# Splitting the FFN columns over the two row groups, with weight loads over 128 partitions

## The chip, the cores and the metric

The kernel runs on one NeuronCore of a Trainium2 chip. The metric is the device time of one execution in microseconds, median over runs. The kernel before takes 527.3 us (525.35 to 528.24, 3 runs). In the profile, PE is the matmul engine (TensorE), PEld its weight loading, DVE is VectorE, ACT is ScalarE, POOL is GpSimd and SP is SyncE, which issues transfers here and computes nothing. "SPq" is SP's instruction queue. The transfers of SP, ACT and POOL travel in different queues (in the page of the kernel before 17.79, 0.52 and 11.80 MB), but those of SP and POOL share the same 16 DMA engines. A packet is the piece of a transfer that the records list one by one; in the new weight loads it is one row of 4608 bytes for one partition.

## The reference

Two residual blocks follow each other on 2048 tokens of 576 values, in bfloat16: a spectral filter after a layer norm, then a gated FFN after a layer norm.

```python
def _A_ref(x, w_r, w_i):                      # S, D = 2048, 576
    X = jnp.fft.rfft2(x.astype(jnp.float32), axes=(-2, -1))
    X = X * (w_r + 1j * w_i)
    return jnp.fft.irfft2(X, s=(S, D), axes=(-2, -1)).astype(jnp.bfloat16)

def _B_ref(x, w_gate, w_up, w_down):          # 576x4608, 576x4608, 4608x576
    return (_gelu(x @ w_gate) * (x @ w_up)) @ w_down

h  = x + _A_ref(_layernorm(x), A_w_r, A_w_i)
h2 = h + _B_ref(_layernorm(h), B_w_gate, B_w_up, B_w_down)
```

## The kernel before

The spectral block is a chain of matmul stages on PE (forward transforms, 16 groups with a 16-point stage on both sides of the filter, an inverse transform), lasting until about 91 us. The FFN then goes through four blocks of 512 tokens. The contraction over 576 values is cut into 9 chunks of 64. A matmul then has 64 rows, and two of them, in the upper and in the lower row group, run at the same time: in the profile below a gate/up matmul of 64 rows and 512 columns takes 108.1 ns, which is 0.211 ns per column, a down matmul of 128 rows and only 288 columns 122.9 ns, 0.427 per column. In the kernel before the gate weights lie in partitions 0 to 63 and the up weights in 64 to 127; one row group computes gate, the other up. For this the normalized input HT is stored twice, so that each chunk is there for both row groups; slots 5 to 8 of HT are copies of slots 0 to 4 in the other half.

```python
# weights: two transfers per 512 columns, each to 64 partitions, rows of 1024 bytes
for j in range(9):
    f0, f1 = 512 * j, 512 * j + 512
    P.dma(POOL, WGU[0:64, :, f0:f1],   wgv[:, :, f0:f1], f"wg{j}", w=[("WG", j, 0)])
    P.dma(SP,   WGU[64:128, :, f0:f1], wuv[:, :, f0:f1], f"wu{j}", w=[("WG", j, 1)])
# WD shares its memory with the spectral stage, so its loads wait for the end of that
for j in range(9):
    P.dma(POOL, WD[:, 4 * j:4 * j + 4, :], wdv[:, 4 * j:4 * j + 4, :], f"wd{j}", w=[("WD", j)])
...
# first FFN block: PE transposes the input, DVE evicts, SP copies into the other half
P.op(DVE, ... v.tensor_copy(HT0[:, 0:5, t0:t1], PS[...]) ...)
P.dma(SP, HT0[0:64, 5:9, t0:t1],   HT0[64:128, 0:4, t0:t1], f"tr{c}", ...)
P.dma(SP, HT0[64:128, 5:9, t0:t1], HT0[0:64, 1:5, t0:t1],   f"tr{c}", ...)
...
def gu(n, tb, f):                    # 36 column tiles f per token block
    b0 = 2 * (n % 3)                 # three pairs of PSUM banks
    for kt in range(9):
        for o in range(2):           # o = 0 gate, upper rows; 1 up, lower rows
            h0, sl = 64 * o, (GT, UT)[o][kt]
            P.op(PE, ... t.matmul(bank(b0 + o), WGU[h0:h0 + 64, kt, 128 * f:128 * f + 128],
                                  HT[h0:h0 + 64, sl, :], start=(kt == 0), stop=(kt == 8)) ...)
    ...
    P.op(ACT, ... GL = gelu(bank b0)); P.op(DVE, ... AT[:, f, :] = GL * bank b0 + 1)
```

SP's queue holds, in this order: the inputs, constants and filter weights, the tables DT and IT for the inverse transform, the nine up transfers, the copies into HT.

Of the kernel before, what the change touches and what calls it, by code (L numbers as in the profile page):

```python
# [4 lines left out]
BF16 = mybir.dt.bfloat16  # L5
# [5 lines left out]
KW = 290  # L11
ZW = 320
FF = 4608
NT = 16
# [268 lines left out]
def _build(nc, A_x, A_w_r, A_w_i, B_w_gate, B_w_up, B_w_down, out):  # L283
# [6 lines left out]
    top = nc.sbuf_top  # L290
    sb = SbufMap(nc, base, top)
    XO = sb.alloc("XO", [128, NT, D], BF16)
    WGU = sb.alloc("WGU", [128, 9, FF], BF16)
    HN = sb.alloc("HN", [128, 2, 640], BF16)
    IDT = sb.alloc("IDT", [128, 128], BF16)
    ST1 = sb.alloc("ST1", [128, NT, 2, 6], F32)
# [39 lines left out]
    YS = sb.alloc("YS", [128, 2, 2, KW], BF16)  # L336
    T1 = sb.alloc("T1", [128, 2, 2, KW], BF16)
    T2 = sb.alloc("T2", [128, 2, 2, KW], BF16)
    ZS = sb.alloc("ZS", [128, 2, 2, ZW], BF16)
    SQ = sb.alloc("SQ", [128, 2, D], BF16)  # L340
    sb.off = v_off
    AT = sb.alloc("AT", [128, 36, 512], BF16)
    HT1 = sb.alloc("HT1", [128, 9, 512], BF16)
    GL = sb.alloc("GL", [128, 2, 512], BF16)
    HTS = (HT0, HT1)

    PS = nc.alloc_psum_tensor("PS", [128, 4096], F32)
# [1 line left out]
    def bank(b, p0=0, p1=128, c0=0, c1=512):  # L349
        return PS[p0:p1, b * 512 + c0:b * 512 + c1]  # L350
# [182 lines left out]
    def st_B(i):  # L533
        g = GORD[i]
        sl = i % 2
        sp_ = 1 if g == 0 else 0
        for b, tabs in ((4, (0, 1)), (5, (1, 2))):
            for o in range(2):
                P.op(PE, lambda t, b=b, o=o, tb=tabs[o], sl=sl, sp_=sp_: t.matmul(bank(b, 0, 128, 0, K2), BT[:, sp_, tb, :], CUS[:, sl, o, 0:K2],  # L539
                                                                              start=(o == 0), stop=(o == 1)),  # L540
                     r=[("CU", sl) if o == 0 else ("SU", sl), "BT"], w=[("PS", b)])
        P.op(ACT, lambda a, sl=sl: a.activation(YS[:, sl, :, 0:K2], banks(4, 2, K2), ACTF.Copy), r=[("PS", 4), ("PS", 5)], w=[("Y", sl)])  # L542
        wk = wkeys[0 if 1 <= g < 9 else 1] + ["Wz", "Yz", "Zz"]
        P.op(DVE, lambda v, g=g, sl=sl: v.tensor_tensor(T1[:, sl, :, :], YS[:, sl, :, :], WS[:, g, :, :], op=ALU.mult), r=[("Y", sl)] + wk, w=[("T1", sl)])  # L544
        for pl in range(2):
            P.op(DVE, lambda v, g=g, sl=sl, pl=pl: v.tensor_tensor(T2[:, sl, pl, :], YS[:, sl, pl, :], WS[:, g, 1 - pl, :], op=ALU.mult),
                 r=[("Y", sl)] + wk, w=[("T2", sl, pl)])
        P.op(DVE, lambda v, sl=sl: v.tensor_tensor(ZS[:, sl, 0, 0:KW], T1[:, sl, 0, :], T1[:, sl, 1, :], op=ALU.subtract), r=[("T1", sl)], w=[("Z", sl, 0)])
        P.op(DVE, lambda v, sl=sl: v.tensor_tensor(ZS[:, sl, 1, 0:KW], T2[:, sl, 0, :], T2[:, sl, 1, :], op=ALU.add), r=[("T2", sl, 0), ("T2", sl, 1)], w=[("Z", sl, 1)])  # L549

    def st_V(i):
        g = GORD[i]
        sl = i % 2
        sp_ = 1 if g == 0 else 0
        zk = [("Z", sl, 0), ("Z", sl, 1), "Zz", "VT"]
        for c in range(2):
            for zp in range(2):
                P.op(PE, lambda t, c=c, zp=zp, sl=sl, sp_=sp_: t.matmul(bank(6, 0, 128, 256 * c, 256 * c + 256), ZS[:, sl, zp, 128 * c:128 * c + 128],  # L558
                                                                        VT[:, sp_, zp, :], start=(zp == 0), stop=(zp == 1)), r=zk, w=[("PS", 6)])
        for t_ in range(2):  # L560
            for zp in range(2):
                P.op(PE, lambda t, t_=t_, zp=zp, sl=sl, sp_=sp_: t.matmul(bank(7, 64 * t_, 64 * t_ + 64, 0, 128), ZS[:, sl, zp, 256:320],  # L562
                                                                         VT[:, sp_, zp, 128 * t_:128 * t_ + 128], start=(zp == 0), stop=(zp == 1)),
                     r=zk, w=[("PS", 7)])
        P.op(ACT, lambda a, g=g: a.activation(V[:, 0:4, :, g, :], bank(6).rearrange("p (k n e) -> p k n e", k=4, n=16), ACTF.Copy),  # L565
             r=[("PS", 6), "Vfree"], w=[("V", g)])
        P.op(DVE, lambda v, g=g: v.tensor_copy(V[:, 4, :, g, :], bank(7, 0, 128, 0, 128).rearrange("p (n e) -> p n e", n=16)),
             r=[("PS", 7), "Vfree"], w=[("Vt", g)])


    P.alias(["ATB", "J0", "J1", "ZD"] + [("ATS", c) for c in range(NT)], ["Vfree"])
    for i in range(NG + 2):
        if i < NG:
            st_D(i)
        if 1 <= i <= NG:
            st_B(i - 1)
        if i >= 2:
            st_V(i - 2)


    wgv = B_w_gate[:, :].rearrange("(t p) f -> p t f", p=64)
    wuv = B_w_up[:, :].rearrange("(t p) f -> p t f", p=64)
    wdv = B_w_down[:, :].rearrange("(c p) d -> p c d", p=128)
    for j in range(9):
        f0, f1 = 512 * j, 512 * j + 512
        P.dma(POOL, WGU[0:64, :, f0:f1], wgv[:, :, f0:f1], f"wg{j}", w=[("WG", j, 0)])
        P.dma(SP, WGU[64:128, :, f0:f1], wuv[:, :, f0:f1], f"wu{j}", w=[("WG", j, 1)])
    P.alias(ukeys + wkeys[0] + wkeys[1] + ["Wz", ("CU", 0), ("CU", 1), ("SU", 0), ("SU", 1)], [("WD", j) for j in range(9)])
    for j in range(9):
        P.dma(POOL, WD[:, 4 * j:4 * j + 4, :], wdv[:, 4 * j:4 * j + 4, :], f"wd{j}", w=[("WD", j)])  # L590
# [52 lines left out]
    def turn_dma(c):  # L643
        hs = c % 2
        q = c // 4
        HT = HTS[q % 2]
        for k in range(9):
            o = 128 * k if k < 5 else 64 + 128 * (k - 5)
            P.dma(SP, HT[:, k, 128 * (c % 4):128 * (c % 4) + 128], HN[:, hs, o:o + 128], f"tr{c}",
                  r=[("HN", hs, 0), ("HN", hs, 1)], w=[("HT", q % 2, c % 4, k)], transpose=True)  # L650
# [27 lines left out]
            turn_pe((c - 7) // 2)  # L678

    fdead = vkeys + ["DT", "IT", ("G", 0), ("G", 1), ("Y", 0), ("Y", 1), "Yz", "Zz", ("SQ", 0), ("SQ", 1)]  # L680
    fdead += [("T1", a) for a in range(2)] + [(n_, a, b_) for n_ in ("T2", "Z") for a in range(2) for b_ in range(2)]
    fnew = ([("AT", f) for f in range(36)] + [("GL", 0), ("GL", 1)] + [("HT", 1, i, k) for i in range(4) for k in range(9)])

    GT = (0, 5, 1, 6, 2, 7, 3, 8, 4)
    UT = (4, 0, 5, 1, 6, 2, 7, 3, 8)

    def gu(n, tb, f):
        b0 = 2 * (n % 3)
        HT = HTS[tb % 2]
        rk = [("HT", tb % 2, i, k) for i in range(4) for k in range(9)] + [("WG", f // 4, i) for i in range(2)]  # L690
        for kt in range(9):
            for o in range(2):
                h0, sl = 64 * o, (GT, UT)[o][kt]
                P.op(PE, lambda t, o=o, h0=h0, kt=kt, sl=sl, f=f, b0=b0, HT=HT: t.matmul(  # L694
                    bank(b0 + o), WGU[h0:h0 + 64, kt, 128 * f:128 * f + 128], HT[h0:h0 + 64, sl, :], start=(kt == 0), stop=(kt == 8)),
                    r=rk, w=[("PS", b0 + o)])
        if n == 0:
            st_N(NT - 1)
            P.alias(fdead, fnew)
        s2 = n % 2  # L700
        P.op(ACT, lambda a, s2=s2, b0=b0: a.activation(GL[:, s2, :], bank(b0), ACTF.Gelu_apprx_tanh), r=[("PS", b0)], w=[("GL", s2)])  # L701
        P.op(DVE, lambda v, s2=s2, b0=b0, f=f: v.tensor_tensor(AT[:, f, :], GL[:, s2, :], bank(b0 + 1), op=ALU.mult),  # L702
             r=[("GL", s2), ("PS", b0 + 1)], w=[("AT", f)])

    def down(tb, p):
        b0 = 6 - 2 * (p % 2)
        c = 4 * tb + p
        for h in range(2):
            for f in range(36):
                P.op(PE, lambda t, b0=b0, h=h, f=f, p=p: t.matmul(bank(b0 + h, 0, 128, 0, 288), AT[:, f, 128 * p:128 * p + 128],  # L710
                                                                  WD[:, f, 288 * h:288 * h + 288], start=(f == 0), stop=(f == 35)),
                     r=[("AT", f), ("WD", f // 4)], w=[("PS", b0 + h)])
            P.op(DVE, lambda v, b0=b0, h=h, p=p, c=c: v.tensor_tensor(OS[:, p % 2, 288 * h:288 * h + 288], bank(b0 + h, 0, 128, 0, 288),  # L713
                                                                      XO[:, c, 288 * h:288 * h + 288], op=ALU.add),
                 r=[("PS", b0 + h), ("X", c)], w=[("OS", p % 2, h)])
            P.dma(SP, ov[:, c, 288 * h:288 * h + 288], OS[:, p % 2, 288 * h:288 * h + 288], f"so{p % 2}{h}", r=[("OS", p % 2, h)], w=[("OUT", p % 2, h)])

    for tb in range(4):
        for f in range(36):
            gu(36 * tb + f, tb, f)  # L720
            if tb == 0 and f == 20:
                ln2_a(3)
                ln2_b(3)
                ln2_c(3)
            if tb < 3 and f % 4 == 3 and f < 16:
                norm(4 * (tb + 1) + f // 4)
                turn_dma(4 * (tb + 1) + f // 4)
        for p in range(4):
            down(tb, p)
    P.op(SP, None, r=[("OUT", i, h) for i in range(2) for h in range(2)])  # L730
# [36 lines left out]
```

## Time and profile before

| what | value | view |
|---|---|---|
| time | 527.3 us | runs |
| span; PE busy | 526.9 us; 96% | page, part 1 |
| one FFN block, gate/up and down | 70.04 and 35.39 us | chain of waits |
| first gate/up matmul starts | 98.8 us | chain of waits |
| PE waits for the copies into HT | 8.1 us | waits |

From the page, the busy share in 40 slices of 13.2 us: each digit is tenths, PEclk is the granted clock in tenths, DMA the share of 16 DMA engines.

```profile
span 526.9 us, 10210 instructions
...
PE   7899898499999999999999999999999999999997
...
PEclk9999999699999999999999999999999999999999
DMA  8999999401110000011100000111000000000000
```

PE is full from slice 9 on; the DMA engines are full until slice 7. The dip of PE and of its clock lies at the border of the two stages. The next lines are from the chain of waits: start, length, what.

```profile
94.94 3.51 DMA HT_69<-HT_69
...
98.81 4.02 PE PS L694 x18
...
207.93 70.04 PE PS L694 x648
277.97 35.39 PE PS L710 x288
```

The first matmul of the FFN is released by a copy into HT. From the second block on there is no gap: 648 matmuls in 70.04 us are 108.1 ns each, two in parallel. The DMA engines in some stretches (the last two figures of a row are the busy share of 16 engines and GB/s):

```profile
core 0: us, PE busy (x) PEld busy (x) DVE busy (x) ACT busy (x) POOL busy (x), PEclk, DMA share, GB/s
20.00:40.00 20.00, 18.81 (x164) 13.48 (x163) 13.23 (x46) 11.16 (x23) 4.49 (x7) 1.00 1.06 215
40.00:60.00 20.00, 20.00 (x178) 14.36 (x176) 15.20 (x57) 12.36 (x25) 0.00 (x0) 1.00 1.06 233
60.00:85.00 25.00, 22.68 (x194) 16.80 (x193) 16.44 (x54) 18.37 (x41) 6.72 (x9) 1.00 1.09 265
85.00:99.00 14.00, 5.89 (x51) 4.33 (x50) 5.17 (x16) 6.04 (x15) 0.00 (x0) 0.83 0.94 223
```

And the issues of transfers, with the median time from issue to landing:

```profile
WGU<-in_B_w_gate_dram POOLq DMA_DIRECT2D x9, 576.0 KB, 25.8
WGU<-in_B_w_up_dram SPq DMA_DIRECT2D x9, 576.0 KB, 31.7
WD<-in_B_w_down_dram POOLq DMA_DIRECT2D x9, 576.0 KB, 18.0
...
DT<-c_dtab SPq DMA_DIRECT2D x1, 720.0 KB, 24.4
...
IT<-c_itab SPq DMA_DIRECT2D x1, 512.0 KB, 28.0
```

They stand in SP's queue ahead of the up weights, whose first packet came at 40.1 us; this will matter.

### The profile page before, as it was taken

The page shows a single profiled execution, that of the slowest core. Times are in us where ns is not written, and L with a number is a line of the kernel's source. Part 1 is how long each engine was busy: PE and PEld are TensorE (multiplying, and loading weights), DVE is VectorE, ACT ScalarE, POOL GpSimd, SP SyncE. Part 2 cuts the span into 40 slices and gives each one's busy share as a digit, 9 for nine tenths or more (in the row PEclk, how much of TensorE's full clock was granted, in tenths as well). Part 3 has the DMA queues.
Part 4 walks back from the last instruction along what each step waited for, and adds up shares of the span by engine and source line. Part 5 has one row for each costly group of instructions (what it writes and reads, how often), then busy time and mean ns, then how long its engine had stood idle before and what let it go on. Part 6 is the DMA issues. An engine that isn't in the chain of part 4 may idle for free.

```text
span 526.9 us, 10210 instructions
## 1 busy us (share of the span) xinstructions
PE 507.8 (96%) x4425; PEld 302.5 (57%) x4427; DVE 184.1 (35%) x428; ACT 152.8 (29%) x285; POOL 29.1 (6%) x49
## 2 busy tenths in 40 slices
PE   7899898499999999999999999999999999999997
PEld 3667576144444777444447774456677744444776
DVE  5677658044433111343331114433311133333111
ACT  5756578042343000223330002333300023333000
POOL 8800130000000000000000000000000000000000
PEclk9999999699999999999999999999999999999999
DMA  8999999401110000011100000111000000000000
GB/s 289 247 208 230 220 268 316 68 11 26 26 25 7 13 18 18 11 26 24 26 9 12 17 18 11 27 27 26 6 12 18 18 1 1 0 1 2 12 18 18
DMA packets 36812, 30.76 MB, mean 58 GB/s; under 512 B 21296, under 2 KB 32752, under 8 KB 36768
## 3 DMA queue, kind: packets, MB, share of 16 engines
q1 hardware_dynamic: 33312, 17.79, 14.8%
q0 software_dynamic: 3312, 11.80, 8.8%
q8 instruction: 35, 0.57, 0.5%
q10 hardware_dynamic: 144, 0.52, 0.3%
q14 instruction: 9, 0.07, 0.1%
HBM read 23.67 MB, written 2.36 MB: 49 GB/s over the span
## 4 chain that ended last, share of the span: by engine, by line
PE 88%; SPq 3%; DVE 3%; DMA 3%; ACT 2%; issue 1%; DVEq 0%; ACTq 0%
PE PS L694 51%; PE PS L710 27%; PE PS L525 4%; PE PS L601 3%; SPq L191 2%; DMA XO<-in_A_x_dram 2%; PE PS L539 1%; SPq L193 1%; PE PS L558 1%; ACT U L453 1%; DMA HT_69<-HT_69 1%; PE PS L610 1%; PE PS L562 1%; DVE XO L613 1%; DMA HT_84<-HN 0%
## 5 line engine op out<-in xcount | busy, mean ns | idle before, releaser
L701 ACT ACTIVATE GL<-PS 128x512 bf16<-128x512 f32 x144 | 85.8, 597 | 294.5 <-PE PS L694 293.0
L702 DVE TENSOR_TENSOR AT<-GL,PS 128x512 bf16<-128x512 bf16 x144 | 98.6, 687 | 167.1 <-ACT GL L701 167.1
L694 PE MATMUL PS<-HT_69,WGU 64*128 64x512 bf16 x1296 | 143.3, 380 | 8.2 <-DMA HT_69<-HT_69 8.1
L710 PE MATMUL PS<-WD,AT 128*128 128x288 bf16 x1152 | 141.8, 286 | 0.0
L694 PE MATMUL PS<-HT_84,WGU 64*128 64x512 bf16 x1296 | 140.2, 376 | 0.0
L710 PEld LDWEIGHTS PS<-WD,AT 128*128 128x128 bf16 x1152 | 112.4, 98 | 29.9 <-issue 1.7
L694 PEld LDWEIGHTS PS<-HT_69,WGU 64*128 64x128 bf16 x1296 | 70.8, 95 | 79.8 <-issue 11.7
L694 PEld LDWEIGHTS PS<-HT_84,WGU 64*128 64x128 bf16 x1296 | 62.6, 94 | 77.1 <-issue 0.5
L713 DVE TENSOR_TENSOR OS<-PS,XO 128x288 bf16<-128x288 f32 x32 | 14.6, 458 | 123.8 <-PE PS L710 123.8
L601 PE MATMUL PS<-DT,V 128*128 128x288 bf16 x160 | 22.0, 286 | 0.5 <-ACT V L565 0.5
L525 PE MATMUL PS<-FT,U 128*128 128x289 bf16 x160 | 22.3, 287 | 0.2 <-ACT U L453 0.2
L613 DVE SCALAR_TENSOR_TENSOR XO<-PS,XO 128x576 bf16<-128x576 f32 x16 | 12.1, 756 | 20.0 <-PE PS L610 19.8
L601 PEld LDWEIGHTS PS<-DT,V 128*128 128x128 bf16 x160 | 15.4, 98 | 4.3 <-issue 0.6
L525 PEld LDWEIGHTS PS<-FT,U 128*128 128x128 bf16 x160 | 14.4, 97 | 5.1 <-issue 0.4
L616 ACT ACTIVATE SQ<-XO 128x576 bf16<-128x576 bf16 x16 | 10.9, 682 | 15.3 <-DVE XO L613 15.1
L639 DVE TENSOR_SCALAR HN<-XO,TM,RS_59 128x576 bf16<-128x576 bf16 (+1 forms) x32 | 10.2, 360 | 8.8 <-DMA HT_84<-HN 6.4
L434 PE MATMUL PS<-ZD 128*128 128x512 bf16 x37 | 10.9, 447 | 1.5 <-POOL ZD L356 1.3
L558 PE MATMUL PS<-VT,ZS 128*128 128x256 bf16 x64 | 9.6, 271 | 2.4 <-DVE ZS L549 1.6
L405 DVE BATCH_NORM_STATS2 ST_53<-XO 128x6 f32<-128x288 bf16 x24 | 9.2, 443 | 5.5 <-DMA XO<-in_A_x_dram 5.5
L544 DVE TENSOR_TENSOR T_79<-YS,WS 128x580 bf16<-128x580 bf16 x16 | 7.4, 460 | 10.4 <-ACT YS L542 10.4
L603 ACT ACTIVATE GS<-PS 128x576 bf16<-128x576 f32 x16 | 10.2, 636 | 2.6 <-PE PS L601 2.6
L542 ACT ACTIVATE YS<-PS 128x578 bf16<-128x578 f32 x16 | 10.5, 655 | 1.5 <-PE PS L539 0.3
(57 smaller groups left out, 171.8 us busy)
## 6 DMA issues: line engine op xcount, KB each, us to landing
WGU<-in_B_w_gate_dram POOLq DMA_DIRECT2D x9, 576.0 KB, 25.8
WGU<-in_B_w_up_dram SPq DMA_DIRECT2D x9, 576.0 KB, 31.7
WD<-in_B_w_down_dram POOLq DMA_DIRECT2D x9, 576.0 KB, 18.0
out_dram<-OS SPq DMA_DIRECT2D x32, 72.0 KB, 1.6
XO<-in_A_x_dram SPq DMA_DIRECT2D x3, 576.0 KB, 8.0
HT_84<-HN SPq DMA_TRANSPOSE x72, 2.4
FT<-c_ftab SPq DMA_DIRECT2D x1, 725.0 KB, 12.5
DT<-c_dtab SPq DMA_DIRECT2D x1, 720.0 KB, 24.4
```

The costliest lines, as they stand in the source:

```text
L191: fn = lambda e: e.dma_start(out_ap, in_ap, transpose=True)
L434: P.op(PE, lambda t: t.matmul(bank(7), ZD[:, 0:128], ZD[:, :], start=True, stop=True), r=["ZD"], w=[("PS", 7)])
L525: P.op(PE, lambda t, b=b, o=o, dt=dt, g=g: t.matmul(bank(b, 0, 128, 0, K2), U[:, dt, g, :, :], FT[:, dt, o, 0:K2], start=(dt == 0), stop=( ...
L558: P.op(PE, lambda t, c=c, zp=zp, sl=sl, sp_=sp_: t.matmul(bank(6, 0, 128, 256 * c, 256 * c + 256), ZS[:, sl, zp, 128 * c:128 * c + 128], V ...
L601: P.op(PE, lambda t, b=b, h=h, kt=kt, c=c: t.matmul(bank(b, 0, 128, 0, 288), V[:, kt, c, :, :], DT[:, kt, 288 * h:288 * h + 288], start=(k ...
L613: P.op(DVE, lambda v, x2=x2, c=c: v.scalar_tensor_tensor(x2, banks(4, 2, 288), 1.0, x2, op0=ALU.mult, op1=ALU.add, accum_out=SB2[:, 0, c:c ...
L616: P.op(ACT, lambda a, sl=sl, c=c: a.activation(SQ[:, sl, :], XO[:, c, :], ACTF.Square, accum_out=SB2[:, 1, c:c + 1]), r=[("X", c)], w=[("S ...
L694: P.op(PE, lambda t, o=o, h0=h0, kt=kt, sl=sl, f=f, b0=b0, HT=HT: t.matmul(bank(b0 + o), WGU[h0:h0 + 64, kt, 128 * f:128 * f + 128], HT[h0 ...
L701: P.op(ACT, lambda a, s2=s2, b0=b0: a.activation(GL[:, s2, :], bank(b0), ACTF.Gelu_apprx_tanh), r=[("PS", b0)], w=[("GL", s2)])
L702: P.op(DVE, lambda v, s2=s2, b0=b0, f=f: v.tensor_tensor(AT[:, f, :], GL[:, s2, :], bank(b0 + 1), op=ALU.mult), r=[("GL", s2), ("PS", b0 + ...
L710: P.op(PE, lambda t, b0=b0, h=h, f=f, p=p: t.matmul(bank(b0 + h, 0, 128, 0, 288), AT[:, f, 128 * p:128 * p + 128], WD[:, f, 288 * h:288 * ...
L713: P.op(DVE, lambda v, b0=b0, h=h, p=p, c=c: v.tensor_tensor(OS[:, p % 2, 288 * h:288 * h + 288], bank(b0 + h, 0, 128, 0, 288), XO[:, c, 28 ...
```

## The change

The intent has two parts. First, the columns are split over the row groups: partitions 0 to 63 hold columns 0 to 2303 of gate and of up, partitions 64 to 127 hold columns 2304 to 4607 of both. Each transfer then fills all 128 partitions in runs of 4608 bytes, where before it filled 64 in runs of 1024. One call of `gu` makes two gate tiles, then two up tiles, in two sets of four PSUM banks. Second, the inverse 16-point stage `st_V` lags three groups behind instead of two, with three slots of ZS. The PSUM banks of `down` and the places where the next block is normalized were adapted to this; the cut below leaves that out.

```diff
-    WGU = sb.alloc("WGU", [128, 9, FF], BF16)
+    WGU = sb.alloc("WGU", [128, 2, 9, FF // 2], BF16)
...
-    ZS = sb.alloc("ZS", [128, 2, 2, ZW], BF16)
+    ZS = sb.alloc("ZS", [128, 3, 2, ZW], BF16)
...
-    for i in range(NG + 2):
+    for i in range(NG + 3):
...
-        if i >= 2:
-            st_V(i - 2)
+        if i >= 3:
+            st_V(i - 3)
...
-    for j in range(9):
-        f0, f1 = 512 * j, 512 * j + 512
-        P.dma(POOL, WGU[0:64, :, f0:f1], wgv[:, :, f0:f1], f"wg{j}", w=[("WG", j, 0)])
-        P.dma(SP, WGU[64:128, :, f0:f1], wuv[:, :, f0:f1], f"wu{j}", w=[("WG", j, 1)])
+    for kt in range(9):
+        for o, src in enumerate((B_w_gate, B_w_up)):
+            a = bass.AP(src.tensor, 64 * kt * FF, [[FF // 2, 2], [FF, 64], [1, FF // 2]])
+            P.dma((POOL, SP)[o], WGU[:, o, kt, :], a, f"wg{o}", w=[("WG", o, kt)])
...
+    def gu(tb, n):                       # 18 calls per token block
+        b0 = 4 * (n % 2)
+        for o in range(2):
+            for kt in range(9):
+                for h in range(2):       # h: row group and half of the columns
+                    h0, sl = 64 * h, (GT, UT)[h][kt]
+                    P.op(PE, ... t.matmul(bank(b0 + 2 * o + h), WGU[h0:h0 + 64, o, kt, 128 * n:128 * n + 128],
+                                          HT[h0:h0 + 64, sl, :], ...),
+                        r=rk + [("WG", o, k) for k in range(9)], ...)
...                                       # gelu and product for f = n and n + 18; GL has four slots
+    FORD = [f for f in range(36) if f % 18 != 17] + [17, 35]     # order of the down matmuls
```

The first gate matmul now waits for all nine gate transfers and the first up matmul for all nine up transfers; before, each tile waited for its own 512 columns.

More of the change, by code (lines that the diff above doesn't have):

```diff
@@ L343, in _build @@
     HT1 = sb.alloc("HT1", [128, 9, 512], BF16)
-    GL = sb.alloc("GL", [128, 2, 512], BF16)
+    GL = sb.alloc("GL", [128, 4, 512], BF16)
     HTS = (HT0, HT1)
@@ L547, in st_B @@
                  r=[("Y", sl)] + wk, w=[("T2", sl, pl)])
-        P.op(DVE, lambda v, sl=sl: v.tensor_tensor(ZS[:, sl, 0, 0:KW], T1[:, sl, 0, :], T1[:, sl, 1, :], op=ALU.subtract), r=[("T1", sl)], w=[("Z", sl, 0)])
-        P.op(DVE, lambda v, sl=sl: v.tensor_tensor(ZS[:, sl, 1, 0:KW], T2[:, sl, 0, :], T2[:, sl, 1, :], op=ALU.add), r=[("T2", sl, 0), ("T2", sl, 1)], w=[("Z", sl, 1)])
+        P.op(DVE, lambda v, sl=sl: v.tensor_tensor(ZS[:, i % 3, 0, 0:KW], T1[:, sl, 0, :], T1[:, sl, 1, :], op=ALU.subtract), r=[("T1", sl)], w=[("Z", i % 3, 0)])
+        P.op(DVE, lambda v, sl=sl: v.tensor_tensor(ZS[:, i % 3, 1, 0:KW], T2[:, sl, 0, :], T2[:, sl, 1, :], op=ALU.add), r=[("T2", sl, 0), ("T2", sl, 1)], w=[("Z", i % 3, 1)])
     def st_V(i):
         g = GORD[i]
-        sl = i % 2
+        sl = i % 3
         sp_ = 1 if g == 0 else 0
@@ L576, in _build @@
             st_B(i - 1)
-        if i >= 2:
-            st_V(i - 2)
-    wgv = B_w_gate[:, :].rearrange("(t p) f -> p t f", p=64)
-    wuv = B_w_up[:, :].rearrange("(t p) f -> p t f", p=64)
+        if i >= 3:
+            st_V(i - 3)
     wdv = B_w_down[:, :].rearrange("(c p) d -> p c d", p=128)
-    for j in range(9):
-        f0, f1 = 512 * j, 512 * j + 512
-        P.dma(POOL, WGU[0:64, :, f0:f1], wgv[:, :, f0:f1], f"wg{j}", w=[("WG", j, 0)])
-        P.dma(SP, WGU[64:128, :, f0:f1], wuv[:, :, f0:f1], f"wu{j}", w=[("WG", j, 1)])
+    for kt in range(9):
+        for o, src in enumerate((B_w_gate, B_w_up)):
+            a = bass.AP(src.tensor, 64 * kt * FF, [[FF // 2, 2], [FF, 64], [1, FF // 2]])
+            P.dma((POOL, SP)[o], WGU[:, o, kt, :], a, f"wg{o}", w=[("WG", o, kt)])
     P.alias(ukeys + wkeys[0] + wkeys[1] + ["Wz", ("CU", 0), ("CU", 1), ("SU", 0), ("SU", 1)], [("WD", j) for j in range(9)])
@@ L680, in _build @@
     fdead = vkeys + ["DT", "IT", ("G", 0), ("G", 1), ("Y", 0), ("Y", 1), "Yz", "Zz", ("SQ", 0), ("SQ", 1)]
-    fdead += [("T1", a) for a in range(2)] + [(n_, a, b_) for n_ in ("T2", "Z") for a in range(2) for b_ in range(2)]
-    fnew = ([("AT", f) for f in range(36)] + [("GL", 0), ("GL", 1)] + [("HT", 1, i, k) for i in range(4) for k in range(9)])
+    fdead += [("T1", a) for a in range(2)] + [(n_, a, b_) for n_ in ("T2", "Z") for a in range(3) for b_ in range(2)]
+    fnew = ([("AT", f) for f in range(36)] + [("GL", i) for i in range(4)] + [("HT", 1, i, k) for i in range(4) for k in range(9)])
@@ L684, in _build @@
     GT = (0, 5, 1, 6, 2, 7, 3, 8, 4)
     UT = (4, 0, 5, 1, 6, 2, 7, 3, 8)
-    def gu(n, tb, f):
-        b0 = 2 * (n % 3)
+    def gu(tb, n):
+        b0 = 4 * (n % 2)
         HT = HTS[tb % 2]
-        rk = [("HT", tb % 2, i, k) for i in range(4) for k in range(9)] + [("WG", f // 4, i) for i in range(2)]
-        for kt in range(9):
-            for o in range(2):
-                h0, sl = 64 * o, (GT, UT)[o][kt]
-                P.op(PE, lambda t, o=o, h0=h0, kt=kt, sl=sl, f=f, b0=b0, HT=HT: t.matmul(
-                    bank(b0 + o), WGU[h0:h0 + 64, kt, 128 * f:128 * f + 128], HT[h0:h0 + 64, sl, :], start=(kt == 0), stop=(kt == 8)),
-                    r=rk, w=[("PS", b0 + o)])
-        if n == 0:
-            st_N(NT - 1)
-            P.alias(fdead, fnew)
-        s2 = n % 2
-        P.op(ACT, lambda a, s2=s2, b0=b0: a.activation(GL[:, s2, :], bank(b0), ACTF.Gelu_apprx_tanh), r=[("PS", b0)], w=[("GL", s2)])
-        P.op(DVE, lambda v, s2=s2, b0=b0, f=f: v.tensor_tensor(AT[:, f, :], GL[:, s2, :], bank(b0 + 1), op=ALU.mult),
-             r=[("GL", s2), ("PS", b0 + 1)], w=[("AT", f)])
+        rk = [("HT", tb % 2, i, k) for i in range(4) for k in range(9)]
+        for o in range(2):
+            for kt in range(9):
+                for h in range(2):
+                    h0, sl = 64 * h, (GT, UT)[h][kt]
+                    P.op(PE, lambda t, o=o, h=h, h0=h0, kt=kt, sl=sl, n=n, b0=b0, HT=HT: t.matmul(
+                        bank(b0 + 2 * o + h), WGU[h0:h0 + 64, o, kt, 128 * n:128 * n + 128], HT[h0:h0 + 64, sl, :], start=(kt == 0), stop=(kt == 8)),
+                        r=rk + [("WG", o, k) for k in range(9)], w=[("PS", b0 + 2 * o + h)])
+            if o == 0 and tb == 0 and n == 0:
+                st_N(NT - 1)
+                P.alias(fdead, fnew)
+            for h in range(2):
+                f = n + 18 * h
+                s4 = 2 * (n % 2) + h
+                if o == 0:
+                    P.op(ACT, lambda a, s4=s4, b=b0 + h: a.activation(GL[:, s4, :], bank(b), ACTF.Gelu_apprx_tanh), r=[("PS", b0 + h)], w=[("GL", s4)])
+                else:
+                    P.op(DVE, lambda v, s4=s4, b=b0 + 2 + h, f=f: v.tensor_tensor(AT[:, f, :], GL[:, s4, :], bank(b), op=ALU.mult),
+                         r=[("GL", s4), ("PS", b0 + 2 + h)], w=[("AT", f)])
@@ L705, in down @@
+    FORD = [f for f in range(36) if f % 18 != 17] + [17, 35]
     def down(tb, p):
-        b0 = 6 - 2 * (p % 2)
         c = 4 * tb + p
         for h in range(2):
-            for f in range(36):
-                P.op(PE, lambda t, b0=b0, h=h, f=f, p=p: t.matmul(bank(b0 + h, 0, 128, 0, 288), AT[:, f, 128 * p:128 * p + 128],
-                                                                  WD[:, f, 288 * h:288 * h + 288], start=(f == 0), stop=(f == 35)),
-                     r=[("AT", f), ("WD", f // 4)], w=[("PS", b0 + h)])
-            P.op(DVE, lambda v, b0=b0, h=h, p=p, c=c: v.tensor_tensor(OS[:, p % 2, 288 * h:288 * h + 288], bank(b0 + h, 0, 128, 0, 288),
-                                                                      XO[:, c, 288 * h:288 * h + 288], op=ALU.add),
-                 r=[("PS", b0 + h), ("X", c)], w=[("OS", p % 2, h)])
+            b = 2 * p + h
+            for i, f in enumerate(FORD):
+                P.op(PE, lambda t, b=b, h=h, f=f, p=p, i=i: t.matmul(bank(b, 0, 128, 0, 288), AT[:, f, 128 * p:128 * p + 128],
+                                                                    WD[:, f, 288 * h:288 * h + 288], start=(i == 0), stop=(i == 35)),
+                     r=[("AT", f), ("WD", f // 4)], w=[("PS", b)])
+            P.op(DVE, lambda v, b=b, h=h, p=p, c=c: v.tensor_tensor(OS[:, p % 2, 288 * h:288 * h + 288], bank(b, 0, 128, 0, 288),
+                                                                    XO[:, c, 288 * h:288 * h + 288], op=ALU.add),
+                 r=[("PS", b), ("X", c)], w=[("OS", p % 2, h)])
@@ L716, in down @@
             P.dma(SP, ov[:, c, 288 * h:288 * h + 288], OS[:, p % 2, 288 * h:288 * h + 288], f"so{p % 2}{h}", r=[("OS", p % 2, h)], w=[("OUT", p % 2, h)])
     for tb in range(4):
-        for f in range(36):
-            gu(36 * tb + f, tb, f)
-            if tb == 0 and f == 20:
+        for n in range(18):
+            gu(tb, n)
+            if tb == 0 and n == 9:
                 ln2_a(3)
@@ L724, in _build @@
                 ln2_c(3)
-            if tb < 3 and f % 4 == 3 and f < 16:
-                norm(4 * (tb + 1) + f // 4)
-                turn_dma(4 * (tb + 1) + f // 4)
+            if tb < 3 and n % 2 == 1 and n < 8:
+                norm(4 * (tb + 1) + n // 2)
+                turn_dma(4 * (tb + 1) + n // 2)
         for p in range(4):
```

## The prediction

> What bounds the kernel now. The page gives a span of 526.9 us with PE busy 96%. By the chain of waits, the FFN matmuls (L694, L710) hold 78%, and from the second token block on they run at a floor: each block takes 70.04 us for 648 gate/up matmuls (108.1 ns each, two row groups overlapping) and 35.39 us for 288 down matmuls (122.9 ns each). The only loose time lies before the FFN and in its first block. (a) PE waits 8.1 us for the copies into HT (view of waits): the last HT eviction ends at 89.45 us, the last copy lands at 98.45, because SP's queue and the 16 DMA engines are full (DMA share 1.05 to 1.13 in the stretches from 20 to 90 us, at only 209 to 243 GB/s from 30 to 60 us, but 319 GB/s from 75 to 90). (b) After that idle time the granted clock is 0.54 from 99 to 105 us, worth about 2.8 us. (c) The inverse stage idles about 1.0 us at its first group. (d) DVE waits on HN cost PE 0.7 us in block one.
>
> What the change leaves. It has the same 2592 gate/up matmuls of 64x512 in alternating row groups, so 70.04 us per block stays; four GL slots and reordered banks only add slack. The down order reads its last two AT tiles last, so no new wait there. The lag of 3 should remove (c), about 1 us, and nothing in the periods of 2.51 us, where PE is full.
>
> What it changes is the weight loads. The intent is good: 1024-byte packets to half the partitions take a median 86 to 89 ns in the trace's packet records (11.7 GB/s per engine), whereas 4608-byte packets of the input load took 178 ns (25.9 GB/s). But the DRAM pattern of the new transfers starts with a dimension of 2. [...]
>
> Cost, an estimate from those durations: up is 9 x 64 packets of 4608 bytes per engine, 576 x 178 ns = 102 us; beside it the same engines carry one or two gate transfers (11 to 23 us) and their share of WD (72 packets, 13 us). Starting near 25 us, up lands at about 150 to 163 us. The HT copies queue behind it on SP, so the first gate matmul starts near 157 us instead of 98.8: all on the critical path, plus 58 us. The remaining 428 us stay, less 1.
>
> Prediction: 584 us, range 556 to 606; faster by over 2%: 0.10, within 2%: 0.15, slower by over 2%: 0.75.
>
> What would show it: DMA share drops to about 2/16 to 3/16 between 45 and 150 us at some 50 GB/s; SP's issues of WGU stall past 100 us; PE idle for 60 us at slice 8 to 11, then released by the HT copies or WGU; blocks two to four unchanged at 105.43 us each.
>
> What would make it wrong: if the transfers spread over all 16 engines after all, the weights land by about 62 us and WD by 83, the HT copies by 93, PE stays warm, and (a) to (d) give back 5 + 2.8 + 1 + 0.6 us: about 518 us, just under 2% faster. If two engines move more than 26 GB/s each, or carry fewer gate transfers, the loss is nearer 40 us.

What the estimate goes on to use, that up runs through two engines, was the author's assumption; the changed kernel bears it out (in e0, from 85 to 135 us, up had two packets in flight for 48.6 of 50 us, and never more). The "one or two gate transfers" beside it are an assumption too, and 72 packets of WD per engine are its 1152 spread evenly over 16; in e0 279 packets of POOL's queue began after 85 us. 102 us for up, 11 to 23 for gate and 13 for WD make 126 to 138 us from 25 us on.

## The result, and the profile after

The changed kernel takes 622.0 us (median of four runs, one of them slow; the three fast ones took 620.85 to 622.14), against 527.8 us for the kernel before in the same rounds: ratio 1.179, interval 1.174 to 1.184. Ratios here are the mean time of one kernel's fast runs over that of the other's of the same rounds, so they are not quite the ratio of the medians quoted. The first profiled run (707.5 us, clock 0.771) is not used. The unaltered kernel was run once more (e0 below): 622.3 us at clock 0.915, which agrees with the fast runs. All lines of "after" are from that run.

From its page, as before (a slice is now 15.5 us):

```profile
span 620.1 us, 10178 instructions
...
PE   7999980000005999999999999999999999999998
...
PEclk9999895555556999999999999999999999999999
DMA  9998951111111011000011100001110000000000
```

PE stands still for more than six slices (102.8 us). The DMA share in those slices is 0.1, not 0.9: the transfers neither finish nor keep the engines busy. From its chain of waits:

```profile
128.43 11.31 SPq L193
...
139.79 20.11 SPq L193
...
188.65 4.85 DMA HT<-HT
...
193.74 3.62 PE PS L694 x18
...
301.19 70.03 PE PS L694 x648
371.23 35.39 PE PS L716 x288
```

The first gate/up matmul starts at 193.74 us instead of 98.81, which is 94.9 us later. The blocks after the first take 70.03 and 35.39 us, as before. The whole loss therefore lies ahead of the FFN: the span grew by 620.1 - 526.9 = 93.2 us. The stretches and issues:

```profile
40.00:60.00 20.00, 19.93 (x176) 14.22 (x175) 15.20 (x57) 12.44 (x24) 0.00 (x0) 1.00 1.01 165
60.00:85.00 25.00, 23.17 (x186) 16.73 (x185) 15.43 (x51) 17.28 (x39) 6.77 (x9) 0.93 0.90 223
85.00:135.00 50.00, 5.93 (x51) 4.34 (x48) 5.41 (x16) 6.27 (x15) 0.00 (x0) 0.59 0.13 52
135.00:180.00 45.00, 0.00 (x0) 0.00 (x0) 0.00 (x0) 0.00 (x0) 0.00 (x0) 0.50 0.15 56
```

```profile
WGU<-in_B_w_gate_dram POOLq DMA_DIRECT2D x9, 576.0 KB, 36.1
WGU<-in_B_w_up_dram SPq DMA_DIRECT2D x9, 576.0 KB
WD<-in_B_w_down_dram POOLq DMA_DIRECT2D x9, 576.0 KB, 118.0
```

From 85 to 135 us the share is 0.13, that is 2 of 16 engines (0.125), at 52 GB/s. The chain shows SP occupied for 11.31 us per up transfer. The packet records of the trace, counted by queue, say the same:

| stretch, us | up packets of 4608 bytes (SP's queue) | median ns | packets of 4608 bytes of POOL's queue |
|---|---|---|---|
| 20 to 49 | 1 | - | 794 |
| 49 to 85 | 263 | about 255 | 1231 |
| 85 to 135 | 552 | 178 | 7 |
| 135 to 187 | 336 | 178 | 241 |

The up weights are 9 x 128 = 1152 packets. From 85 to 135 us two engines can begin 2 x 50 / 0.178 = 562 packets, and 552 began: two engines, busy without a break. The overlap of the same records agrees: up had two packets in flight for 48.6 of these 50 us, and never more. From 49 to 85 us it had two for 32.6 of 36 us, while POOL's queue most often had 14, which makes 16 together. One transfer of 128 packets over two engines is 64 x 177 ns = 11.3 us, the same 11.31 us that SP spends on one issue.

### The profile page after: what moved, and what is told of

It is laid out like the page before. It is cut to its first block, busy times and chain, and to the rows that moved or that the text cites. A ratio compares the mean times of both kernels' runs of the same rounds, so it can differ in the third digit from the quotient of the medians.

```text
span 705.3 us, 10180 instructions
## 1 busy us (share of the span) xinstructions
PE 611.0 (87%) x4427; PEld 320.9 (46%) x4427; DVE 178.7 (25%) x428; ACT 147.0 (21%) x285; POOL 29.7 (4%) x49
## 4 chain that ended last, share of the span: by engine, by line
PE 72%; SPq 26%; DMA 1%; issue 0%; DVE 0%; DVEq 0%
PE PS L694 48%; SPq L193 26%; PE PS L716 24%; DMA HT_69<-HT_69 1%; PE PS L609 0%; DVE OS L719 0%; DVEq L258 0%
## 5 line engine op out<-in xcount | busy, mean ns | idle before, releaser
L694 PE MATMUL PS<-HT_69,WGU 64*128 64x512 bf16 x1296 | 175.2, 441 | 86.6 <-DMA HT_69<-HT_69 86.6
L716 PE MATMUL PS<-WD,AT 128*128 128x288 bf16 x1152 | 168.4, 315 | 0.0
L694 PE MATMUL PS<-HT_84,WGU 64*128 64x512 bf16 x1296 | 165.9, 425 | 0.0
L694 PEld LDWEIGHTS PS<-HT_69,WGU 64*128 64x128 bf16 x1296 | 70.2, 106 | 190.5 <-issue 143.1
L704 ACT ACTIVATE GL<-PS 128x512 bf16<-128x512 f32 x144 | 78.1, 594 | 377.3 <-PE PS L694 377.3
L706 DVE TENSOR_TENSOR AT<-GL,PS 128x512 bf16<-128x512 bf16 x144 | 92.5, 684 | 239.7 <-PE PS L694 237.0
L716 PEld LDWEIGHTS PS<-WD,AT 128*128 128x128 bf16 x1152 | 119.1, 104 | 50.0 <-issue 2.1
L694 PEld LDWEIGHTS PS<-HT_84,WGU 64*128 64x128 bf16 x1296 | 66.9, 103 | 98.5 <-issue 17.5
L600 PE MATMUL PS<-DT,V 128*128 128x288 bf16 x160 | 28.0, 338 | 0.5 <-ACT V L565 0.5
L525 PE MATMUL PS<-FT,U 128*128 128x289 bf16 x160 | 27.7, 333 | 0.0
L539 PE MATMUL PS<-CUS,BT 128*128 128x289 bf16 x64 | 13.0, 336 | 0.0
L531 ACT ACTIVATE CUS<-PS 128x289 bf16<-128x289 f32 x16 | 6.6, 414 | 20.7 <-PE PS L525 20.7
```

The costliest lines, as they stand in the source:

```text
L525: P.op(PE, lambda t, b=b, o=o, dt=dt, g=g: t.matmul(bank(b, 0, 128, 0, K2), U[:, dt, g, :, :], FT[:, dt, o, 0:K2], start=(dt == 0), stop=( ...
L539: P.op(PE, lambda t, b=b, o=o, tb=tabs[o], sl=sl, sp_=sp_: t.matmul(bank(b, 0, 128, 0, K2), BT[:, sp_, tb, :], CUS[:, sl, o, 0:K2], start= ...
L600: P.op(PE, lambda t, b=b, h=h, kt=kt, c=c: t.matmul(bank(b, 0, 128, 0, 288), V[:, kt, c, :, :], DT[:, kt, 288 * h:288 * h + 288], start=(k ...
L694: P.op(PE, lambda t, o=o, h=h, h0=h0, kt=kt, sl=sl, n=n, b0=b0, HT=HT: t.matmul(bank(b0 + 2 * o + h), WGU[h0:h0 + 64, o, kt, 128 * n:128 * ...
L704: P.op(ACT, lambda a, s4=s4, b=b0 + h: a.activation(GL[:, s4, :], bank(b), ACTF.Gelu_apprx_tanh), r=[("PS", b0 + h)], w=[("GL", s4)])
L706: P.op(DVE, lambda v, s4=s4, b=b0 + 2 + h, f=f: v.tensor_tensor(AT[:, f, :], GL[:, s4, :], bank(b), op=ALU.mult), r=[("GL", s4), ("PS", b0 ...
```

## The experiments

Theory A, an assumption that these runs test: the DRAM pattern of the new transfers starts with a dimension of 2, and this confines each transfer to two DMA engines; SP's transfers go through two in all, and the copies into HT stand behind them. Rivals: B, the new waits (all nine transfers before the first matmul); C, transfers over 128 partitions in long rows are slow in themselves. All results are correct unless said otherwise.

| run | median us | ratio to before | interval | first gate/up matmul, us |
|---|---|---|---|---|
| changed kernel | 622.0 | 1.179 | 1.174 to 1.184 | 193.7 (e0) |
| e1_halves | 523.3 | 0.993 | 0.987 to 0.998 | 93.1 |
| e1_again (the same) | 524.4 | 0.994 | 0.991 to 0.998 | 94.2 |
| e2_up_halves | 546.4 | 1.036 | 1.030 to 1.042 | 119.7 |
| e3_gate_halves | 603.6 | 1.144 | 1.139 to 1.150 | 173.9 |
| g1_128rows (wrong) | 518.4 | 0.982 | 0.979 to 0.985 | 92.8 |
| f4_short_runs | 524.8 | 0.995 | 0.992 to 0.997 | 95.3 |
| f7_ht_act | 614.9 | 1.165 | 1.162 to 1.168 | 171.9, but see there |
| k1_tables_act | 621.9 | 1.180 | 1.175 to 1.186 | 192.0 |
| f1_lag3 (on the kernel before) | 527.4 | 1.000 | 0.998 to 1.002 | 96.9 |
| h2_opposite | 523.9 | 0.993 | 0.990 to 0.996 | 94.8 |
| h4_opp_split | 521.3 | 0.989 | 0.985 to 0.992 | 92.2 |

### e0: the changed kernel once more

> The changed kernel unaltered, once more, because its first profile fell in the slow state. Both theories: about 622 us. In a fast profile the first gate/up matmul should start near 185 us (it did at 192 us in the slow one, where the weights alone set it), and blocks two to four should take 105.4 us each as before; if they don't, something besides the weight loads costs time.

It took 622.3 us; its lines are shown above. The matmul started at 193.7 us, later than the 185 expected, and the blocks were at their floor.

### e1: each transfer cut in two halves

```diff
-            a = bass.AP(src.tensor, 64 * kt * FF, [[FF // 2, 2], [FF, 64], [1, FF // 2]])
-            P.dma((POOL, SP)[o], WGU[:, o, kt, :], a, f"wg{o}", w=[("WG", o, kt)])
+            for h in range(2):
+                a = bass.AP(src.tensor, 64 * kt * FF + h * (FF // 2), [[FF, 64], [1, FF // 2]])
+                P.dma((POOL, SP)[o], WGU[64 * h:64 * h + 64, o, kt, :], a, f"wg{o}", w=[("WG", o, kt, h)])
```

> Each weight transfer is cut into its two halves of 64 partitions, so that the DRAM pattern starts with a dimension of 64 instead of 2; rows of 4608 bytes, layout, order, waits and the lag of 3 stay. Theory A (the leading 2 confines each transfer to two DMA engines): DMA share back near 1.0 up to about 85 us, first gate/up matmul by 93 to 99 us, time 516 to 525 us. Rival B (the new waits: the first gate matmul needs all nine gate transfers, the first up matmul all nine up transfers, and long rows of one kt are a bad order): over 580 us.

The same bytes go to the same places under the same waits (the matmuls now name both halves of each transfer), and the time is 523.3 us. Stretches and chain:

```profile
20.00:40.00 20.00, 19.69 (x173) 14.25 (x174) 13.97 (x47) 12.11 (x24) 7.37 (x15) 1.00 1.05 248
40.00:60.00 20.00, 19.93 (x176) 14.27 (x175) 15.20 (x57) 12.36 (x24) 0.00 (x0) 1.00 1.03 243
60.00:85.00 25.00, 23.17 (x185) 16.71 (x183) 15.31 (x51) 16.98 (x39) 6.73 (x9) 0.93 1.03 288
```

```profile
90.76 2.13 DMA HT<-HT
...
93.14 2.12 PE PS L695 x18
```

The engines are full again (1.03 to 1.05 of 16), and the matmul starts at 93.1 us. Rival B falls: e1 keeps the waits for all nine transfers and is not slow.

### g1: one transfer over 128 partitions, with another leading dimension

```diff
-            a = bass.AP(src.tensor, 64 * kt * FF, [[FF // 2, 2], [FF, 64], [1, FF // 2]])
+            a = bass.AP(src.tensor, 56 * kt * FF, [[FF, 128], [1, FF // 2]])     # wrong rows, on purpose
```

> Wrong results on purpose. The changed kernel with one thing altered: each weight transfer still fills 128 partitions with 4608 bytes each in one piece, but reads 128 consecutive rows of half the columns, so that the DRAM pattern starts with 128 instead of 2. Theory A (the leading 2 alone confines the transfers): not slower than the halves, 515 to 525 us, with a DMA share near 1 up to 60 us. Rival C (one transfer over all 128 partitions in long rows is itself slow, and the halves helped because they are smaller): near 622 us.

The result is wrong. The time is 518.4 us, and the stretches read:

```profile
20.00:40.00 20.00, 19.88 (x173) 14.16 (x171) 13.96 (x48) 11.82 (x23) 2.67 (x6) 1.00 1.05 374
40.00:60.00 20.00, 19.93 (x177) 14.22 (x175) 15.20 (x57) 12.44 (x24) 0.00 (x0) 1.00 0.66 266
```

Rival C falls: transfers of 128 partitions and 4608 bytes are the fastest of all if their DRAM pattern starts with 128. The only thing that differs from the changed kernel is the pattern on the DRAM side, and with it which rows are read (some of them twice, and only the first half of the columns). A packet takes as long as in the changed kernel, 181 against 178 ns; what differs is how many are in flight. Together with the share of 2/16 in the changed kernel this shows theory A in its main point. Between 40 and 60 us the packets of g1 took a median 181 ns, those of e1 318 ns; all up weights of g1 were under way by 53.9 us, those of e1 by 77.5. A real layout that has both the split columns and a leading 128 was not found: partition 64 + r would need an address 2304 columns after partition r, and no single stride does that.

### e2 and e3: only one of the two queues mended

In e2 only the up transfers are halved as in e1, in e3 only the gate transfers.

> Only the up transfers (SP's queue) are cut in halves; the gate transfers (POOL's queue) keep the leading 2. Theory A[...]: nearly the whole loss goes, 517 to 535 us. If POOL's transfers shared one pair too, or if the loss were not from SP's, it would stay over 580 us.

> Only the gate transfers (POOL) are cut in halves; the up transfers (SP) keep the leading 2. Theory A: the up transfers still take 1152 packets of 178 ns on two engines, 102.5 us; the gate load on these two engines falls from 128 packets each to 72, so 5 to 15 us of the loss go: 605 to 617 us. Rival B: no change, 622 us.

e3, with up still whole, took 603.6 us: of the 99 us between the changed kernel and e1, 80 are there with the up transfers alone (603.6 - 523.3). It is 1 us below its range, so mending gate saved a little more than expected (the 128 gate packets per engine in the expectation, two whole transfers, were the author's assumption). e2 took 546.4 us, which is 23 us over e1 and above its range: the gate transfers on POOL's queue were expected to cost next to nothing. What the expectation assumed for this, about the engines that the transfers of each queue get, is shown by no run. The chain of e2:

```profile
92.84 26.50 DMA HT<-HT
...
119.68 3.77 PE PS L701 x18
```

The last copy into HT, issued at 92.2 us, landed 26.5 us later. POOL's queue is why it was late, as far as the records go: its weights were under way until 118.5 us, against 90.1 in e1. In e2 only 123 gate packets began between 14 and 45 us, beside 634 of up; in e1 it was 753 beside 119. So POOL's queue fell behind early and ended late. From 28 to 45 us it had 1.9 packets in flight on average, beside 13.7 of SP's; in the changed kernel, with the same POOL transfers, it most often had 14 from 49 to 85 us. Why it began so few packets beside SP's is open.

### f7: the copies into HT in another queue

```diff
-        P.dma(SP, HT0[0:64, 5:9, t0:t1], HT0[64:128, 0:4, t0:t1], f"tr{c}", ...)
-        P.dma(SP, HT0[64:128, 5:9, t0:t1], HT0[0:64, 1:5, t0:t1], f"tr{c}", ...)
+        P.dma(ACT, HT0[0:64, 5:9, t0:t1], HT0[64:128, 0:4, t0:t1], f"tr{c}", ...)
+        P.dma(ACT, HT0[64:128, 5:9, t0:t1], HT0[0:64, 1:5, t0:t1], f"tr{c}", ...)
```

> The changed kernel with the copies into HT issued from ScalarE's queue instead of SP's. In the changed kernel the last up packet is over near 181 us but the first gate/up matmul starts at 193.7 us, because the copies stand behind the up transfers in SP's queue. Theory: 8 to 12 us of the loss are this tail, so 610 to 615 us, start near 182 to 186 us. If the weights themselves land that late, no change: 620 to 624 us.

614.9 us, 7 us less. (The expectation put the last up packet near 181 us; in the records it begins at 186.5.) What PE's gate/up matmuls waited for, from the view of the weights' tile:

```profile
  DMA WGU<-in_B_w_gate_dram: 78.2, 1
  DMA WGU<-in_B_w_up_dram: 24.2, 2
```

Now no copy holds PE: it waits for the last gate transfer until 171.9 us, runs the 18 matmuls of the first two gate tiles, and waits again for the last up transfer until 187.8 (PE 11.9 us and its weight loading 12.2, together the 24.2 of the view). The copies behind the up transfers are therefore worth about 7 us; the rest of the loss is the weights themselves.

### k1: the tables out of SP's queue

```diff
-    P.dma(SP, DT[...], dram["DTAB"][:, :], "dt", w=["DT"])        # ahead of the up transfers; IT and IDT too
...
     idle_mm(3)
+    P.dma(ACT, DT[...], dram["DTAB"][:, :], "dt", w=["DT"])       # IT and IDT too
```

> The changed kernel with the three table transfers (DT, IT, IDT) moved out of SP's queue, where they stand ahead of the up transfers, to ScalarE's queue at about 21 us. The prediction let up start near 25 us; in the changed kernel its first packet came at 49.0 us. If it waits for the tables ahead of it in SP's queue, the first packet now comes at 23 to 32 us, the last near 168 to 176 us instead of 186.5, and the time falls by 8 to 20 us, to 602 to 614 us. If the two engines are simply occupied by the gate transfer until 45 us or so, the start and the time hardly move: 618 to 623 us.

The first up packet came at 33.0 us instead of 49.0, and the last at 178.8 instead of 186.5, but the time did not move (621.9 us) and the matmul started at 192.0 us. The start was the wrong place to look. Of the 1152 up packets only 42 had begun by 49 us, and at the end the copies into HT took longer to land, 8.45 us for the last one, where it had been 4.85:

```profile
183.31 8.45 DMA HT<-HT
...
192.00 4.03 PE PS L694 x18
```

The last packet of POOL's queue began at 190.0 us, in the changed kernel at 191.3. This fits two engines that are busy from the start, with up, tables, gate and WD to carry: then the sum of their work sets the end, and its order changes little. That both queues share the same two engines is an inference, since the records name no engine.

### f4: rows of 1152 bytes

```diff
-    for kt in range(9):                      # as in e1
+    for j in range(4):
         for o, src in enumerate((B_w_gate, B_w_up)):
             for h in range(2):
-                a = bass.AP(src.tensor, 64 * kt * FF + h * (FF // 2), [[FF, 64], [1, FF // 2]])
-                P.dma((POOL, SP)[o], WGU[64 * h:64 * h + 64, o, kt, :], a, ...)
+                f0 = 576 * j
+                a = src[:, :].rearrange("(t p) f -> p t f", p=64)[:, :, (FF // 2) * h + f0:(FF // 2) * h + f0 + 576]
+                P.dma((POOL, SP)[o], WGU[64 * h:64 * h + 64, o, :, f0:f0 + 576], a, ...)
```

> The kernel with halved transfers, but in rows of 1152 bytes (576 columns of all nine chunks per transfer) instead of 4608. If long rows are what the halves gain over the kernel before, this returns to 526 to 529 us with 8 us of waiting for the copies into HT. If the row length counts little, 520 to 525 us like the halves.

524.8 us, ratio 0.995. It can't be told from e1 (0.993 and 0.994). Where a transfer fills 64 partitions, four times longer rows gain nothing that these runs resolve.

### f1: the lag of 3 alone

The kernel before, with the lag and the third slot of ZS and nothing else.

> The kernel before with only the lag of 3 in the inverse stage (and three slots of ZS). By the prediction it removes one wait of 1.0 us at the first group and nothing in the periods: 526.3 us against 527.5, ratio 0.997 to 0.999. If the lag shortened the periods, 16 x 0.1 us and more would go: ratio 0.994 or less.

The ratio is 1.000. The stage itself did get shorter. PE's timeline for the first matmul of the stage and the first after it, in the kernel before:

```profile
21.61 2.63 PE L525 MATMUL PS<-FT,U 128*128 128x289 bf16 x20 [0.19 <-ACT U L453]
...
65.24 2.00 PE L601 MATMUL PS<-DT,V 128*128 128x288 bf16 x15 [0.50 <-ACT V L565]
```

and in f1:

```profile
22.32 2.63 PE L525 MATMUL PS<-FT,U 128*128 128x289 bf16 x20
...
64.67 2.61 PE L601 MATMUL PS<-DT,V 128*128 128x288 bf16 x20 [0.50 <-ACT V L565]
```

From 65.24 - 21.61 = 43.63 us it went to 64.67 - 22.32 = 42.35 us, 1.3 us less; in the changed kernel (e0) the same stretch takes 63.91 - 21.57 = 42.34 us. But in this kernel the FFN starts when the copies into HT land, and those wait for the DMA engines, not for PE (PE still waited 6.8 us for them in f1). So the gain was not seen in the time.

### e1_again, h2, h4: a version that beats both

h2 is meant to let POOL and SP fill opposite halves of the partitions at the same time; h4 also issues the second of the two copies into HT from ACT.

```diff
-            for h in range(2):
+            for h in (o, 1 - o):                                                   # h2 and h4
...
-        P.dma(SP, HT0[64:128, 5:9, t0:t1], HT0[0:64, 1:5, t0:t1], f"tr{c}", ...)
+        P.dma(ACT, HT0[64:128, 5:9, t0:t1], HT0[0:64, 1:5, t0:t1], f"tr{c}", ...)   # h4
```

> The kernel with halved transfers unaltered, with more rounds, beside its two variants: 520 to 524 us, ratio to the kernel before 0.985 to 0.995.

> The halves, but SP's queue takes the upper half of the partitions first, so that POOL's and SP's transfers fill opposite halves at the same time. With both queues on the same 64 partitions the 4608-byte packets took 305 to 324 ns, against 178 to 188 ns where one transfer filled all 128. If this is because both queues write to the same half, the packets fall to 180 to 250 ns and the time to 517 to 521 us; if it is because each single transfer covers only half of the partitions, packets stay near 310 ns and the time at 520 to 524 us.

> The same with the second of the two HT copies issued from ScalarE's queue, so that the two are issued at the same time. The wait between the last eviction and the first gate/up matmul (2.9 us with the halves) shrinks by one issue of 0.6 us: within the noise of the variant beside it, at best 0.999 of it.

e1 again gave 0.994. h2 gave 0.993, with 4608-byte packets at a median 314 ns from 40 to 60 us (e1_again: 321): the order of the halves made no difference that these runs resolve. This fits that each transfer over only 64 partitions is slow by itself, but it does not show it: the records name no partition, and the two queues started 16 us apart, so it is not known that they filled opposite halves at the same time. The kernel before points the same way: there gate always fills the lower half and up the upper one, and its full engines moved 215 to 233 GB/s from 20 to 60 us, though in shorter rows. h4 gave 0.989, the best correct version, 521.3 us. Its interval overlaps that of h2, so its gain over h2, larger than expected, is not settled. In the chains, h2 first:

```profile
88.84 5.70 DMA HT<-HT
...
94.79 4.02 PE PS L695 x18
```

```profile
89.42 2.51 DMA HT<-HT
...
92.17 2.12 PE PS L695 x18
```

In h4 the first 18 matmuls took 2.12 us, in h2 4.02. PE had waited 0.8 us for the copy in h4 and 5.4 us in h2, and the granted clock from 90 to 100 us was 0.66 on average in h2, 1.00 in h4. In the kernel before it was 0.50 from 95 to 99 us, at the end of the wait of 8.1 us, and 0.54 from 99 to 105. The 18 matmuls took 2.12 us after waits of 0.8 and 1.8 us (h4, e1), and 4.02 us after waits of 5.4 and 8.1 us (h2, the kernel before). The profile of h4 is also one in which the weights came earlier (packets at 271 to 275 ns from 40 to 60 us), so the split of the copies is not shown to be the cause.

## Why the prediction was wrong

The direction and the mechanism were right, the size was not: 622.0 us lies outside 556 to 606, and the loss was 94 us where 57 had been forecast. The step that failed is the sum of the work on the two engines: from 25 us on it was to take 126 to 138 us, up to the last up packet, and it took 161.5 (186.5 - 25); points 4 to 6 take it apart.

1. **Right: the mechanism.** That a leading 2 means two engines was an assumption. The traces agree for SP's queue: the share was 0.13 with a leading 2 (85 to 135 us), and 1.05 with 64 (e1) or 128 (g1; both 20 to 40 us). That the nine transfers kept to the same two fits the 552 packets in 50 us and SP's 11.31 us per issue. On changing engines they could have overlapped, as POOL's gate transfers with the same pattern did: 794 of their packets began from 20 to 49 us, where two at a time, at 178 ns each, would give 2 x 29 / 0.178 = 326. The overlap count shows two up packets in flight and no more, so two engines at a time; the records name no engine, so that they were always the same two is not shown directly.
2. **Right: all of it on the critical path, and blocks two to four unchanged** (70.03 and 35.39 us).
3. **Right: 518 us if the transfers used 16 engines.** g1 took 518.4 us. The halves only reach 523 to 524. A likely reason is that the full engines moved about 245 GB/s in halves (e1, 20 to 60 us) and 374 in g1 (20 to 40 us), but no run isolates it: the two profiled runs, the fastest of e1 and the slowest of g1, start their first gate/up matmul within 0.3 us of each other.
4. **Failed: "576 x 178 ns = 102 us" and "one or two gate transfers (11 to 23 us) and their share of WD (72 packets, 13 us)".** This sum is where the size went wrong. The 178 ns come from the input load at the very start. The number of packets was about right (after 85 us POOL's queue began 279 of them; a gate transfer of 128 and two engines' share of WD, 144, are 272), their time was not: while all 16 engines were at work, up to 85 us, up packets took about 255 ns and POOL's about 350 (40 to 60 us). Per engine, half of the 263 up packets at 77 ns too little are 10 us, and 64 gate packets at 172 ns too little are 11 us. The tables' packets on the two engines (an estimated 16 each, DT's and IT's 256 spread evenly over 16) were left out, some 5 us. Together these are 26 us, which on top of 138, the sum with two gate transfers, gives 164, against the 161.5 measured. This is arithmetic with medians, not an experiment, and it assumes that one of the two gate transfers used these engines before 49 us.
5. **Failed: "Starting near 25 us".** The first up packet came at 49.0 us. The profile before had said so: the tables ahead of up in SP's queue landed at 19.5 + 24.4 = 43.9 and 20.2 + 28.0 = 48.2 us, and up's first packet came at 40.1. Counted from 49.0 us, the up load took 137.5 us, within the 126 to 138 of the sum, so the late start looks like the whole error. k1 speaks against that: there up started 16 us earlier, its load took 146 us, and the time did not change. The likely reason is that the two engines had other work in that time.
6. **Failed: "the first gate matmul starts near 157 us", with no time of their own for the copies behind the weights.** They came 7 us after the last up packet (186.5 to 193.7 us); f7 shows that taking them out of SP's queue is worth 7 us of time.
7. **Partly failed: (c), the lag.** The stage is 1.3 us shorter (1.0 forecast), but the time is not (f1): the gain ran into the wait for the copies.
8. **Right in size, where PE hardly waits: (b) and (d).** Block one of the gate/up stage, from its first matmul to the first down matmul, took 172.48 - 98.81 = 73.67 us before and 163.63 - 93.14 = 70.49 us in e1, 3.2 us less; 2.8 + 0.6 had been forecast for the granted clock of 0.54 and for what DVE's waits on HN cost PE. In e1_again, where PE had waited 4.8 us for the copies, it took 72.0 us: the gain depends on that wait.

Still open: why POOL's gate transfers with a leading 2 cost 23 us in e2 (against e1), and why from 85 to 135 us only 7 packets of POOL's queue began beside 552 of SP's (28 beside 552 in k1), where in e3, from 85 to 97.75 us, 65 began beside 73. In the changed kernel 241 of POOL's followed from 135 to 187 us, and POOL had issued its last transfer by 69; whether its packets stood ready at the two engines all that time is not recorded.

## What to carry to other kernels

Look at the first dimension of a transfer's pattern before anything else (the runs here varied it on the DRAM side): a leading 2 put a 5.3 MB load on two engines and cost 80 us here, though rows were longer and all 128 partitions covered. In the profile of e0 such a load shows as a DMA share of 2/16 (0.13 from 85 to 135 us) with a queue that never empties, and it also held up the copies issued after it in its queue, by some 7 us (f7). When you size such a load, add up all the work on the engines that carry it, at packet times taken from the busy stretch, and read from the old profile when the transfers ahead of it in its queue land.
